# Weight loads as plain 128-partition reads, and ring loads placed in the space freed longest ago, in a two-layer decode kernel

## The chip, the cores and the metric

The kernel runs on one core of a Trainium2 chip. The metric is the device time of one execution in microseconds (us), the median of several runs. Of this kernel a profile gives the span from the first to the last instruction, some 2 to 3 us shorter than the device time of the same run (2660.8 for 2663.54 us before).

## The reference

Two layers of decoding with batch 2 and one new token. The same weights and the same caches serve both layers.

```python
x = A_x                                     # (2, 1, 576)
for layer in range(2):
    x = x + A(layernorm(x))                 # attention: 32 heads of 128, 16384 cached keys per head
    x = x + Bm(layernorm(x))                # mixer + MLP: x1 = x + shifted @ w2; x1 + gelu(ln(x1) @ w3) @ w4
# A:  q = x @ wq (576 x 4096); p = softmax(q K^T / sqrt(128)); o = p V; o @ wo (4096 x 576)
# Bm: w2 576 x 576, w3 576 x 4608, w4 4608 x 576; with one token the shifted term is zero
```

K and V hold 2 x 32 x 16384 x 128 bfloat16 values each: 64 "units" (batch x head) of 4.2 MB of K and 4.2 MB of V. They are read once in each layer, except for the last two units of layer 0, which stay in SBUF and are used first in layer 1. About 1.1 GB are moved in all.

## The kernel before

All loads of K, V, wq, w2, w3 and w4 go through one SBUF buffer of 12 slots of 16384 B a partition. The SP queue issues them in a fixed order. A K or V half (2 MB) fills one slot. A load may start when whatever lay in its place has been read. The place is chosen while the program is built, in program order:

```python
class Ring:                                             # (cut)
    def _place(self, n, aligned):
        p = self.at                                     # always the next address
        if aligned:
            p = -(-p // self.slot) * self.slot
        for _ in range(4 * len(self.live) + 4):
            if p + n > self.size:
                p = 0
            kept = [t for t in self.live if t["keep"] and t["off"] < p + n and p < t["off"] + t["n"]]
            if not kept:
                return p                                # skips tiles kept for layer 1, nothing else
            p = max(t["off"] + t["n"] for t in kept)
            ...
    def pump(self):
        while self.queue:
            key, n, src, aligned = self.queue[0]        # strictly in order
            p = self._place(n, aligned)
            if p is None:
                return
            under = [t for t in self.live if t["off"] < p + n and p < t["off"] + t["n"]]
            if not all(t["done"] for t in under):
                return                                  # that very place must be done
            ...
```

The matrices wq and w3 have 576 rows: four blocks of 128 and a tail of 64 rows. The tail is read as two loads, left columns to partitions 0 to 63, right columns to partitions 64 to 127:

```python
def krows(w, k, cut):
    n = w.shape[1]
    if k < self.KT - 1:
        ap = w[k * 128:(k + 1) * 128, :]
        return n, [lambda e, v: e.dma_start(v, ap)]
    a0, a1 = w[k * 128:D, 0:cut], w[k * 128:D, n - cut:n]
    return cut, [lambda e, v: e.dma_start(v[0:64, 0:cut], a0),
                 lambda e, v: e.dma_start(v[64:128, 0:cut], a1)]
...
# load order in each layer: K of unit i, then V of unit i-1, ...; at the end V 62, V 63, w3 (4 + tail), w4 (4 pieces),
# then (layer 0) wq of the next layer (4 + tail) and layer 1's K 61, K 60, V 61, K 59, V 60, ...
if l == 0 and i == 2:
    ap = self.w2.rearrange("(p r) n -> p (r n)", p=96)       # w2 on 96 partitions
```

Of the kernel before, what the change touches and what calls it, by code (L numbers as in the profile page):

```python
# [4 lines left out]
ALU = mybir.AluOpType  # L5
# [140 lines left out]
class Ring:  # L146
# [3 lines left out]
    def __init__(self, s, buf, size, slot):  # L150
        self.s, self.buf, self.size, self.slot = s, buf, size, slot
        self.at = 0
        self.live = []
        self.tiles = {}
        self.queue = []

# [3 lines left out]
    def _place(self, n, aligned):  # L160
        p = self.at
        if aligned:
            p = -(-p // self.slot) * self.slot
        for _ in range(4 * len(self.live) + 4):
            if p + n > self.size:
                p = 0
            kept = [t for t in self.live if t["keep"] and t["off"] < p + n and p < t["off"] + t["n"]]
            if not kept:
                return p
            p = max(t["off"] + t["n"] for t in kept)  # L170
            if aligned:
                p = -(-p // self.slot) * self.slot
        return None

    def pump(self):
        while self.queue:
            key, n, src, aligned = self.queue[0]
            p = self._place(n, aligned)
            if p is None:
                return  # L180
            under = [t for t in self.live if t["off"] < p + n and p < t["off"] + t["n"]]
            if not all(t["done"] for t in under):
                return
# [3 lines left out]
            t = dict(off=p, n=n, done=False, keep=False,  # L187
                     res=[("tile", key, part, self.s.n_dma) for part in range(len(src))])
            self.live.append(t)
            self.tiles[key] = t  # L190
            self.at = p + n
# [8 lines left out]
    def keep(self, key):  # L200
        self.tiles[key]["keep"] = True

    def done(self, key):
        t = self.tiles.pop(key)
        t["done"], t["keep"] = True, False
        self.pump()


class Decode:
# [6 lines left out]
    FJ = 4  # L216
    W4_PIECES = (3, 3, 2, 1)

    def __init__(self, nc, A_x, K, V, wq, wo, w2, w3, w4, out):
# [13 lines left out]
        self.FA0 = (self.FA + 1) // 2  # L233
# [12 lines left out]
        self.ring = Ring(self.s, self.ringbuf, self.NSLOT * self.slot, self.slot)  # L246
# [4 lines left out]
        self.cinv = sb("cinv", [128, 1], FP32)  # L251
        self.cone = sb("cone", [128, 1], FP32)
        self.ceps = sb("ceps", [128, 1], FP32)
# [4 lines left out]
        self.m1 = sb("m1", [128, 2], FP32)  # L258
        self.m2 = sb("m2", [128, 2], FP32)
        self.m = sb("m", [128, 2], FP32)  # L260
        self.bias = sb("bias", [128, 2], FP32)
# [11 lines left out]
        self.xnh = sb("xnh", [128, 2, B], BF16)  # L273
        self.xsum = sb("xsum", [128, KT, B], FP32)
        self.zero = sb("zero", [128, B], BF16)
        self.st = sb("st", [128, 2, B], FP32)
        self.var = sb("var", [128, B], FP32)
        self.rstd = sb("rstd", [128, B], FP32)
# [5 lines left out]
        self.gt = sb("gt", [128, MB], BF16)  # L284
# [20 lines left out]
    def plan(self):  # L305
        ring, B, H, D, TB = self.ring, self.B, self.H, self.D, self.TB
# [6 lines left out]
        def krows(w, k, cut):  # L313


            n = w.shape[1]
            if k < self.KT - 1:
                ap = w[k * 128:(k + 1) * 128, :]
                return n, [lambda e, v: e.dma_start(v, ap)]  # L319
            a0, a1 = w[k * 128:D, 0:cut], w[k * 128:D, n - cut:n]  # L320
            return cut, [lambda e, v: e.dma_start(v[0:64, 0:cut], a0),  # L321
                         lambda e, v: e.dma_start(v[64:128, 0:cut], a1)]
# [6 lines left out]
        def want_wq(l):  # L329
            for k in range(self.KT):  # L330
                n, src = krows(self.wq, k, H * 64)
# [6 lines left out]
        for l in range(2):  # L338
            order = self.order[l]
            skip = self.kept if l == 1 else set()  # L340
            for i, u in enumerate(order):
# [3 lines left out]
                if l == 0 and i == 2:  # L345
                    ap = self.w2.rearrange("(p r) n -> p (r n)", p=96)
                    ring.want(("w2",), 6 * D, [lambda e, v: e.dma_start(v[0:96, :], ap)])
# [3 lines left out]
            for k in range(self.KT):  # L351
                n, src = krows(self.w3, k, self.FA0 * self.FJ * 128)
# [26 lines left out]
    def release(self, kind, l, u, h):  # L379
        k = self.key(kind, l, u, h)  # L380
        if u in self.kept and l == 0:
            self.ring.keep(k)
        else:
            self.ring.done(k)


    def build(self):
# [3 lines left out]
        def consts(g):  # L391
# [4 lines left out]
            g.memset(self.xnh[:, :, :], 0.0)  # L396
            return g.memset(self.ident[:, :], 0.0)
        self.pool(consts, w=["ident", "consts", "xnh"])
# [8 lines left out]
                                           scalar2=None, op0=ALU.mult), r=["ident"], w=["identS"])  # L407
        xt = self.misc[:, :].bitcast(BF16)
# [59 lines left out]
    def k_matmuls(self, kind, l, out, pname, groups, over, pick):  # L468
# [4 lines left out]
        for k in range(self.KT):  # L473
# [10 lines left out]
            def halves(pe, w=w):  # L484
                for g in range(G - over):
                    for j in range(J):
                        m = g * J + j
                        at, rhs = out[:, m * B:(m + 1) * B], self.xnh[:, :, :]
                        if g < over:
                            at = bass.AP(tensor=at.tensor, offset=at.offset,  # L490
                                         ap=[list(at.ap[0]), [over * J * B, 2], [1, B]])
                        else:
                            at, rhs = out[:, (m + over * J) * B:(m + over * J + 1) * B], rhs[:, 1, :]
                        ins = pe.matmul(at, lhsT=pick(w, g, j), rhs=rhs, start=False, stop=True,
# [10 lines left out]
    def split_last(self):  # L505


        low = self.misc[0:64, 280:280 + self.B]
        self.pe(lambda pe: pe.matmul(low, lhsT=self.ident[64:128, 64:128], rhs=self.xn[64:128, self.KT - 1, :],
# [279 lines left out]
```

## Time and profile before

| | before |
|---|---|
| median of the runs | 2665.4 us |
| span of the profile | 2660.8 us |
| DMA rate in the steady state | 425 GB/s, one 2 MB load every 4.9 us |
| DMA rate over the span | 414 GB/s |

Lines of the page of the kernel before. "DMA" is the busy share of the 16 DMA engines in tenths in each of 40 slices, "GB/s" what they moved; the line of q8 has packets, MB and the share of 16 engines' time; the last line is the chain that ended last, by engine.

```profile
span 2660.8 us, 74381 instructions
...
DMA  9999999999999999999869999999999999999997
GB/s 388 425 426 426 425 424 426 426 426 425 425 425 426 425 425 425 425 425 425 338 249 425 424 427 424 426 425 425 425 426 425 426 425 425 427 425 425 425 425 293
...
q8 instruction: 270, 4.42, 0.7%
...
DMA 75%; DVE 24%; PE 1%; issue 0%; SPq 0%; ACT 0%; DVEq 0%
```

The DMA engines are busy nearly everywhere, so time is bytes over rate plus whatever slows or stops them. They move less at the start, in slices 20 and 21 (the layer boundary) and at the end.

The issues of the SP queue at the boundary of the kernel before: start and length in us, line, what is loaded, how many.

```profile
start us, us, engine line op out<-in xcount [idle before <-releaser]
...
1340.47 14.89 SPq L311 DMA_DIRECT2D ring<-in_A_k_cache_dram  x4
1394.23 0.81 SPq L311 DMA_DIRECT2D ring<-in_A_v_cache_dram  x2
1395.08 7.80 SPq L311 DMA_DIRECT2D ring<-in_A_k_cache_dram  x2
```

Four loads of K (units 61 and 60) are issued up to 1355 us. The next load, V of unit 61, is issued at 1394.23 us. Nothing is issued for 39 us. The waits of SP before (total us, times, longest) say for what:

```profile
engine line waited for: us in total, times, longest us
...
SPq L311 <- PE tps L606: 398.3, 76, 38.9
...
SPq L327 <- PE sps L480: 28.6, 2, 27.8
```

The longest wait for "PE tps" is 38.9 us: PE's transposes of K, that is, a K tile that has to be read before its slot can be taken. The last wait is w4 standing behind w3.

Four stretches of the kernel before: the first tail of wq, the first tail of w3 as the leading DMA engines reach it, the second tail of wq, and the hole. The columns at the end are the granted TensorE clock, the DMA share and GB/s.

```profile
core 0: us, PE busy (x) PEld busy (x) DVE busy (x) ACT busy (x) POOL busy (x), PEclk, DMA share, GB/s
11.00:17.00 6.00, 2.59 (x80) 2.37 (x80) 0.02 (x1) 0.00 (x0) 0.00 (x0) 1.00 1.03 350
1290.00:1302.00 12.00, 6.49 (x170) 5.97 (x167) 10.03 (x12) 6.24 (x10) 0.00 (x0) 0.78 0.99 358
1344.00:1356.00 12.00, 4.95 (x141) 4.56 (x138) 0.59 (x4) 0.28 (x1) 0.00 (x0) 0.50 1.02 324
1376.00:1394.00 18.00, 13.63 (x294) 13.13 (x291) 16.77 (x23) 10.20 (x19) 0.00 (x0) 0.62 0.07 18
```

The trace also records when each of the 16 engines finished its share of each load. I call the time from the first to the last engine's landing the spread. It is 0.4 us for the first load, 5 us at 200 us, 11 us at 550 us and 28 us at the end of layer 0; there, half of the engines lag by 24 us or more, five hardly at all and the other three by 2 to 13 us. In layer 1 it grows to 28 us again. The laggards' last landing is the moment that counts for the consumer.

### The profile page before, as it was taken

The page shows a single profiled execution, that of the slowest core. Times are in us where ns is not written, and L with a number is a line of the kernel's source. Part 1 is how long each engine was busy: PE and PEld are TensorE (multiplying, and loading weights), DVE is VectorE, ACT ScalarE, POOL GpSimd, SP SyncE. Part 2 cuts the span into 40 slices and gives each one's busy share as a digit, 9 for nine tenths or more (in the row PEclk, how much of TensorE's full clock was granted, in tenths as well). Part 3 has the DMA queues.
Part 4 walks back from the last instruction along what each step waited for, and adds up shares of the span by engine and source line. Part 5 has one row for each costly group of instructions (what it writes and reads, how often), then busy time and mean ns, then how long its engine had stood idle before and what let it go on. Part 6 is the DMA issues. An engine that isn't in the chain of part 4 may idle for free.

```text
span 2660.8 us, 74381 instructions
## 1 busy us (share of the span) xinstructions
PE 1570.0 (59%) x34580; PEld 1474.1 (55%) x34580; DVE 1994.1 (75%) x2753; ACT 1098.3 (41%) x1681; POOL 0.9 (0%) x11
## 2 busy tenths in 40 slices
PE   5556556655565655665567556556555555655655
PEld 5555555555555555555556555555555555555554
DVE  5777877777777777777568777777877777777774
ACT  3334434434434443443235434434434433443441
POOL 0000000000000000000000000000000000000000
PEclk7666666666666666666666666666666666666665
DMA  9999999999999999999869999999999999999997
GB/s 388 425 426 426 425 424 426 426 426 425 425 425 426 425 425 425 425 425 425 338 249 425 424 427 424 426 425 425 425 426 425 426 425 425 427 425 425 425 425 293
DMA packets 87085, 1102.65 MB, mean 414 GB/s; under 512 B 9108, under 2 KB 17304, under 8 KB 20216
## 3 DMA queue, kind: packets, MB, share of 16 engines
q1 hardware_dynamic: 78072, 1088.47, 97.0%
q10 hardware_dynamic: 8704, 9.44, 1.0%
q8 instruction: 270, 4.42, 0.7%
q14 instruction: 39, 0.32, 0.0%
HBM read 1097.87 MB, written 0.00 MB: 413 GB/s over the span
## 4 chain that ended last, share of the span: by engine, by line
DMA 75%; DVE 24%; PE 1%; issue 0%; SPq 0%; ACT 0%; DVEq 0%
DMA ring<-in_A_k_cache_dram 69%; DVE sd L639 15%; DVE prod L636 9%; DMA ring<-in_A_v_cache_dram 4%; DMA ring<-in_B_w_dram 1%; DMA ring<-in_A_wq_dram 1%; PE misc L657 0%; PE ops L684 0%; PE misc L519 0%; PE sps L480 0%; SPq L319 0%; PE misc L446 0%; PE misc L448 0%; DVE bias L659 0%; SPq L321 0%
## 5 line engine op out<-in xcount | busy, mean ns | idle before, releaser
L639 DVE TENSOR_REDUCE sd<-prod 128x8 f32<-128x1024 bf16 x1024 | 1249.4, 1220 | 35.4
L610 ACT ACTIVATE ktsb<-tps 128x1024 bf16<-128x1024 bf16 x1024 | 992.1, 1028 | 453.0 <-PE tps L606 447.9
L606 PE MATMUL tps<-ident,ring 128*128 128x128 bf16 x8192 | 830.2, 268 | 289.9 <-DMA ring<-in_A_k_cache_dram 289.9
L636 DVE TENSOR_TENSOR prod<-ring,qb 128x1024 bf16<-128x1024 bf16 x1024 | 699.1, 683 | 230.8 <-DMA ring<-in_A_k_cache_dram 220.1
L606 PEld LDWEIGHTS tps<-ident,ring 128*128 128x128 bf16 x8192 | 676.1, 123 | 314.5 <-DMA ring<-in_A_k_cache_dram 306.7
L684 PE MATMUL ops<-p,ring 128*128 128x1 bf16 x16384 | 469.5, 165 | 518.7 <-DMA ring<-in_A_v_cache_dram 509.3
L684 PEld LDWEIGHTS ops<-p,ring 128*128 128x128 bf16 x16384 | 448.4, 102 | 539.4 <-DMA ring<-in_A_v_cache_dram 529.2
L593 ACT ACTIVATE qb<-misc 128x128 bf16<-128x128 f32 x128 | 35.5, 278 | 1016.2 <-PE misc L591 1016.2
L624 PE MATMUL sps<-qt,ktsb 128*128 128x1 bf16 x8192 | 350.1, 166 | 92.3 <-ACT ktsb L610 83.8
L624 PEld LDWEIGHTS sps<-qt,ktsb 128*128 128x128 bf16 x8192 | 313.0, 102 | 132.5 <-ACT ktsb L610 131.0
L659 DVE TENSOR_REDUCE bias<-misc 128x1 f32<-128x128 f32 x128 | 37.3, 292 | 290.6 <-PE misc L657 290.6
L657 PE MATMUL misc<-identS,m 128*128 128x128 f32 x256 | 95.3, 476 | 34.8 <-DVE m L651 34.8
L657 PEld LDWEIGHTS misc<-identS,m 128*128 128x128 f32 x256 | 69.9, 333 | 36.7 <-DVE m L651 36.7
L519 PE MATMUL misc<-otn,wobuf 128*128 128x2 bf16 x320 | 13.6, 167 | 99.8 <-DVE otn L703 99.8
L519 PEld LDWEIGHTS misc<-otn,wobuf 128*128 128x128 bf16 x320 | 11.0, 105 | 102.7 <-DVE otn L703 102.7
L670 ACT ACTIVATE p<-sps,bias 128x64 bf16<-128x64 f32 x128 | 40.7, 318 | 23.5 <-DVE bias L659 23.5
L670 ACT ACTIVATE p<-sd,bias 128x64 bf16<-128x64 f32 x128 | 45.4, 355 | 0.0
L591 PE MATMUL misc<-ident,qt 128*128 128x128 bf16 x128 | 34.9, 272 | 11.7 <-DVE xa L713 7.8
L480 PE MATMUL sps<-xn,ring 128*128 128x2 bf16 x544 | 18.3, 169 | 16.7 <-DMA ring<-in_A_wq_dram 11.8
L647 DVE TENSOR_REDUCE m<-sps 128x1 f32<-128x64 f32 x128 | 27.6, 215 | 0.0
L670 ACT ACTIVATION_READ_ACCUMULATOR p<-sps,bias 128x1 f32 x128 | 27.1, 212 | 0.0
L480 PEld LDWEIGHTS sps<-xn,ring 128*128 128x128 bf16 x544 | 17.4, 112 | 17.6 <-DMA ring<-in_A_wq_dram 10.1
(70 smaller groups left out, 205.9 us busy)
## 6 DMA issues: line engine op xcount, KB each, us to landing
ring<-in_A_k_cache_dram SPq DMA_DIRECT2D x252, 2048.0 KB, 47.4
ring<-in_A_v_cache_dram SPq DMA_DIRECT2D x252, 2048.0 KB, 51.1
ring<-in_B_w_dram SPq DMA_DIRECT2D x10, 1152.0 KB, 48.1
wobuf<-in_A_wo_dram ACTq DMA_DIRECT2D x32, 288.0 KB, 15.3
ring<-in_A_wq_dram SPq DMA_DIRECT2D x8, 1024.0 KB, 11.6
ring<-in_B_w_dram SPq DMA_DIRECT2D x4, 1728.0 KB, 38.8
ring<-in_B_w_dram SPq DMA_DIRECT2D x4, 320.0 KB, 41.5
ring<-in_B_w_dram SPq DMA_DIRECT2D x2, 576.0 KB, 17.4
```

The costliest lines, as they stand in the source:

```text
L480: ins = pe.matmul(out[:, m * B:(m + 1) * B], lhsT=pick(w, g, j), rhs=self.xn[:, k, :], start=(k == 0 and m == 0), stop=False, skip_group_c ...
L591: self.pe(lambda pe: pe.matmul(self.misc[:, 0:128], lhsT=bcast(self.qt[:, u:u + 1], 128), rhs=self.ident[:, :], start=True, stop=True), r= ...
L593: self.act(lambda a: a.activation(out=self.qb[q][:, :], in_=self.misc[:, 0:128], func=ACT.Copy), r=["P:misc"], w=[f"qb{q}"])
L606: ins = pe.transpose(self.tps[b][:, j * 128:(j + 1) * 128], kt[:, (j0 + j) * 128:(j0 + j + 1) * 128], self.ident[:, :])
L610: self.act(lambda a: a.activation(out=self.ktsb[k][:, :, :].rearrange("p a b -> p (a b)"), in_=self.tps[b][:, :], func=ACT.Copy), r=[f"P:t ...
L624: ins = pe.matmul(self.sps[sp][:, col:col + 1], lhsT=self.ktsb[k][:, j, :], rhs=self.qt[:, u:u + 1], start=True, stop=True)
L636: self.dve(lambda v: v.tensor_tensor(out=self.prod[d][:, :, :], in0=k3, in1=bcast_mid(self.qb[q][:, :], self.CH), op=ALU.mult), r=[*res, f ...
L639: self.dve(lambda v: v.tensor_reduce(out=self.sd[q][:, o:o + self.CH], in_=self.prod[d][:, :, :], axis=AX.X, op=ALU.add), r=[f"prod{d}"], ...
L657: self.pe(lambda pe: pe.matmul(self.misc[:, 128:256], lhsT=bcast(self.m[:, q:q + 1], 128), rhs=self.identS[:, :], start=True, stop=True), ...
L659: self.dve(lambda v: v.tensor_reduce(out=self.bias[:, q:q + 1], in_=self.misc[:, 128:256], axis=AX.X, op=ALU.max, negate=True), r=["P:misc ...
L670: self.act(lambda a, c0=c0, c1=c1, src=src, part=part: a.activation(out=self.p[q][:, c0:c1], in_=src, func=ACT.Exp, bias=self.bias[:, q:q ...
L684: ins = pe.matmul(self.ops[g][:, col:col + 1], lhsT=vt[:, j * 128:(j + 1) * 128], rhs=self.p[q][:, h * self.TB + j:h * self.TB + j + 1], s ...
```

## The change

Two intents. First, a load is placed in whatever free space was freed longest ago, instead of the next address. Second, all weights are read as plain 128-partition loads: the 64-row tails as two partitions a row, w2 as 128 partitions x 4 rows and a rest of 64 rows (74 KB, still on 64 partitions), and w3 and w4 in groups of 3 for 4, so that the halves of the tail come out even. A selector matrix and a parity vector spread the last 64 values of the activations to the new tail layout. The rest makes room in SBUF.

```diff
-class Ring:
+class Arena:
     def _place(self, n, aligned):
-        p = self.at
-        ... (next address, skipping kept tiles)
+        best = None
+        if aligned:
+            starts = range(0, self.size - n + 1, self.slot)
+        else:
+            starts = sorted({0} | {t["off"] for t in self.live} | {t["off"] + t["n"] for t in self.live})
+        for p in starts:
+            if p + n > self.size:
+                continue
+            under = [t for t in self.live if t["off"] < p + n and p < t["off"] + t["n"]]
+            if all(t["done"] for t in under):
+                age = max([t["done"] for t in under], default=0)
+                if best is None or age < best[0]:
+                    best = (age, p, under)
+        return best
...
-    FJ = 4
-    W4_PIECES = (3, 3, 2, 1)
+    FJ = 3
+    W4_PIECES = (5, 4, 2, 1)
...
             if k < self.KT - 1:
                 ap = w[k * 128:(k + 1) * 128, :]
-                return n, [lambda e, v: e.dma_start(v, ap)]
-            a0, a1 = w[k * 128:D, 0:cut], w[k * 128:D, n - cut:n]
-            return cut, [lambda e, v: e.dma_start(v[0:64, 0:cut], a0),
-                         lambda e, v: e.dma_start(v[64:128, 0:cut], a1)]
+            else:
+                n //= 2
+                ap = w[k * 128:D, :].rearrange("r (c n) -> (r c) n", c=2)
+            return n, [lambda e, v: e.dma_start(v, ap)]
...
-                    ap = self.w2.rearrange("(p r) n -> p (r n)", p=96)
-                    ring.want(("w2",), 6 * D, [lambda e, v: e.dma_start(v[0:96, :], ap)])
+                    n = 128 * (self.KT - 1)
+                    w2a, w2b = self.w2[0:n, :].rearrange("(p r) n -> p (r n)", p=128), self.w2[n:D, :]
+                    ring.want(("w2",), KT * D, [lambda e, v: e.dma_start(v[:, 0:(KT - 1) * D], w2a),
+                                                lambda e, v: e.dma_start(v[0:64, (KT - 1) * D:KT * D], w2b)])
... (selector, parity, small tiles merged, matmuls of the tail)
```

More of the change, by code (lines that the diff above doesn't have):

```diff
@@ L143, in bcast_mid @@
     return bass.AP(tensor=ap.tensor, offset=ap.offset, ap=[list(ap.ap[0]), [0, n], list(ap.ap[1])])
-class Ring:
+class Arena:
     def __init__(self, s, buf, size, slot):
         self.s, self.buf, self.size, self.slot = s, buf, size, slot
-        self.at = 0
         self.live = []
@@ L155, in __init__ @@
         self.queue = []
+        self.n_done = 0
     def want(self, key, n, src, aligned=True):
@@ L160, in _place @@
     def _place(self, n, aligned):
-        p = self.at
+        best = None
         if aligned:
-            p = -(-p // self.slot) * self.slot
-        for _ in range(4 * len(self.live) + 4):
+            starts = range(0, self.size - n + 1, self.slot)
+        else:
+            starts = sorted({0} | {t["off"] for t in self.live} | {t["off"] + t["n"] for t in self.live})
+        for p in starts:
             if p + n > self.size:
-                p = 0
-            kept = [t for t in self.live if t["keep"] and t["off"] < p + n and p < t["off"] + t["n"]]
-            if not kept:
-                return p
-            p = max(t["off"] + t["n"] for t in kept)
-            if aligned:
-                p = -(-p // self.slot) * self.slot
-        return None
+                continue
[5 more added lines that the diff above has]
+        return best
     def pump(self):
@@ L177, in pump @@
             key, n, src, aligned = self.queue[0]
-            p = self._place(n, aligned)
-            if p is None:
+            best = self._place(n, aligned)
+            if best is None:
                 return
-            under = [t for t in self.live if t["off"] < p + n and p < t["off"] + t["n"]]
-            if not all(t["done"] for t in under):
-                return
+            _, p, under = best
             self.queue.pop(0)
@@ L186, in pump @@
             self.live = [t for t in self.live if t not in under]
-            t = dict(off=p, n=n, done=False, keep=False,
-                     res=[("tile", key, part, self.s.n_dma) for part in range(len(src))])
+            t = dict(off=p, n=n, done=0, res=[("tile", key, part, self.s.n_dma) for part in range(len(src))])
             self.live.append(t)
             self.tiles[key] = t
-            self.at = p + n
             view = self.buf[:, p:p + n]
@@ L198, in get @@
         return self.buf[:, t["off"]:t["off"] + t["n"]], t["res"]
-    def keep(self, key):
-        self.tiles[key]["keep"] = True
     def done(self, key):
         t = self.tiles.pop(key)
-        t["done"], t["keep"] = True, False
+        self.n_done += 1
+        t["done"] = self.n_done
         self.pump()
@@ L232, in __init__ @@
         self.FA = self.MT // self.FJ
-        self.FA0 = (self.FA + 1) // 2
         assert sum(self.W4_PIECES) == self.FA
@@ L245, in __init__ @@
         self.ringbuf = sb("ring", [128, self.NSLOT * self.slot], BF16)
-        self.ring = Ring(self.s, self.ringbuf, self.NSLOT * self.slot, self.slot)
+        self.ring = Arena(self.s, self.ringbuf, self.NSLOT * self.slot, self.slot)
         self.ktsb = [sb(f"ktsb{i}", [128, self.CH, 128], BF16) for i in range(self.NKT)]
@@ L250, in __init__ @@
         self.identS = sb("identS", [128, 128], FP32)
-        self.cinv = sb("cinv", [128, 1], FP32)
-        self.cone = sb("cone", [128, 1], FP32)
-        self.ceps = sb("ceps", [128, 1], FP32)
         self.qt = sb("qt", [128, self.U], BF16)
@@ L257, in __init__ @@
         self.sd = [sb(f"sd{i}", [128, self.TB], FP32) for i in range(2)]
-        self.m1 = sb("m1", [128, 2], FP32)
-        self.m2 = sb("m2", [128, 2], FP32)
-        self.m = sb("m", [128, 2], FP32)
-        self.bias = sb("bias", [128, 2], FP32)
+        small = sb("small", [128, 11 + 4 * B], FP32)
+        self.cinv, self.cone, self.ceps = small[:, 0:1], small[:, 1:2], small[:, 2:3]
+        self.m1, self.m2, self.m, self.bias = (small[:, 3 + 2 * i:5 + 2 * i] for i in range(4))
+        self.st = small[:, 11:11 + 2 * B].rearrange("p (a b) -> p a b", a=2)
+        self.var, self.rstd = small[:, 11 + 2 * B:11 + 3 * B], small[:, 11 + 3 * B:11 + 4 * B]
         self.wobuf = sb("wobuf", [128, self.GH, self.D], BF16)
@@ L273, in __init__ @@
         self.xnh = sb("xnh", [128, 2, B], BF16)
+        self.sel = sb("sel", [128, 128], BF16)
+        self.par = sb("par", [128, 2], FP32)
         self.xsum = sb("xsum", [128, KT, B], FP32)
         self.zero = sb("zero", [128, B], BF16)
-        self.st = sb("st", [128, 2, B], FP32)
-        self.var = sb("var", [128, B], FP32)
-        self.rstd = sb("rstd", [128, B], FP32)
         MB = self.MT * B
@@ L283, in __init__ @@
         self.zr = g1[:, 0:MB]
-        self.gt = sb("gt", [128, MB], BF16)
+        self.gt = self.prod[0][:, :, :].rearrange("p a b -> p (a b)")[:, 6 * MB:7 * MB]
         self.rows = self.prod[1][:, :, :].rearrange("p a b -> p (a b)")[:, 0:self.D]
@@ L305, in plan @@
     def plan(self):
-        ring, B, H, D, TB = self.ring, self.B, self.H, self.D, self.TB
+        ring, B, H, D, KT, TB = self.ring, self.B, self.H, self.D, self.KT, self.TB
         def kv(src, u, h):
@@ L311, in kv, with krows @@
             return [lambda e, v: e.dma_start(v, ap)]
-        def krows(w, k, cut):
+        def krows(w, k):
             n = w.shape[1]
@@ L330, in want_wq @@
             for k in range(self.KT):
-                n, src = krows(self.wq, k, H * 64)
+                n, src = krows(self.wq, k)
                 ring.want(("wq", l, k), n, src, aligned=(k == 0 and l == 0))
@@ L351, in plan @@
             for k in range(self.KT):
-                n, src = krows(self.w3, k, self.FA0 * self.FJ * 128)
+                n, src = krows(self.w3, k)
                 ring.want(("w3", l, k), n, src, aligned=(k == 0))
@@ L379, in release @@
     def release(self, kind, l, u, h):
-        k = self.key(kind, l, u, h)
-        if u in self.kept and l == 0:
-            self.ring.keep(k)
-        else:
-            self.ring.done(k)
+        if l == 1 or u not in self.kept:
+            self.ring.done(self.key(kind, l, u, h))
     def build(self):
@@ L395, in consts @@
             g.memset(self.zero[:, :], 0.0)
-            g.memset(self.xnh[:, :, :], 0.0)
             return g.memset(self.ident[:, :], 0.0)
-        self.pool(consts, w=["ident", "consts", "xnh"])
+        self.pool(consts, w=["ident", "consts"])
         self.pool(lambda g: g.affine_select(out=self.ident[:, :], in_=self.ident[:, :], compare_op=ALU.not_equal,
@@ L407, in build @@
                                            scalar2=None, op0=ALU.mult), r=["ident"], w=["identS"])
+        up = self.ident[64:128, 64:128]
+        self.dve(lambda v: v.tensor_copy(out=self.sel[64:128, :].rearrange("p (r c) -> p r c", c=2),
+                                         in_=bass.AP(tensor=up.tensor, offset=up.offset,
+                                                     ap=[list(up.ap[0]), [1, 64], [0, 2]])), r=["ident"], w=["sel"])
+        self.dve(lambda v: v.tensor_reduce(out=self.par[:, :],
+                                           in_=self.ident[:, :].rearrange("p (r c) -> p c r", c=2), axis=AX.X,
+                                           op=ALU.add), r=["ident"], w=["par"])
         xt = self.misc[:, :].bitcast(BF16)
@@ L466, in layernorm, with k_matmuls @@
                  r=["xc", "rstd"], w=[dname])
-    def k_matmuls(self, kind, l, out, pname, groups, over, pick):
+    def k_matmuls(self, kind, l, out, pname, groups, pick):
         G, J = groups
@@ L484, in halves @@
             def halves(pe, w=w):
-                for g in range(G - over):
+                for g in range(G // 2):
                     for j in range(J):
                         m = g * J + j
-                        at, rhs = out[:, m * B:(m + 1) * B], self.xnh[:, :, :]
-                        if g < over:
-                            at = bass.AP(tensor=at.tensor, offset=at.offset,
-                                         ap=[list(at.ap[0]), [over * J * B, 2], [1, B]])
-                        else:
-                            at, rhs = out[:, (m + over * J) * B:(m + over * J + 1) * B], rhs[:, 1, :]
-                        ins = pe.matmul(at, lhsT=pick(w, g, j), rhs=rhs, start=False, stop=True,
+                        at = out[:, m * B:(m + 1) * B]
+                        at = bass.AP(tensor=at.tensor, offset=at.offset,
+                                     ap=[list(at.ap[0]), [G // 2 * J * B, 2], [1, B]])
+                        ins = pe.matmul(at, lhsT=pick(w, g, j), rhs=self.xnh[:, :, :], start=False, stop=True,
                                         skip_group_check=True)
@@ L505, in split_last @@
     def split_last(self):
-        low = self.misc[0:64, 280:280 + self.B]
-        self.pe(lambda pe: pe.matmul(low, lhsT=self.ident[64:128, 64:128], rhs=self.xn[64:128, self.KT - 1, :],
-                                     start=True, stop=True), r=["xn", "ident"], w=["P:misc"])
-        def copies(v):
-            v.tensor_copy(out=self.xnh[64:128, 1, :], in_=self.xn[64:128, self.KT - 1, :])
-            return v.tensor_copy(out=self.xnh[0:64, 0, :], in_=low)
-        self.dve(copies, r=["P:misc", "xn"], w=["xnh"])
+        B = self.B
+        twice = self.misc[:, 280:280 + B]
+        self.pe(lambda pe: pe.matmul(twice, lhsT=self.sel[64:128, :], rhs=self.xn[64:128, self.KT - 1, :],
+                                     start=True, stop=True), r=["xn", "sel"], w=["P:misc"])
+        self.dve(lambda v: v.tensor_tensor(
+            out=self.xnh[:, :, :], in0=bcast_mid(twice, 2),
+            in1=bass.AP(tensor=self.par[:, :].tensor, offset=self.par[:, :].offset,
+                        ap=[list(self.par[:, :].ap[0]), [1, 2], [0, B]]), op=ALU.mult),
+            r=["P:misc", "par"], w=["xnh"])
     def d_matmuls(self, pe, out, w, rhs, first, last):
@@ L523, in q_proj @@
     def q_proj(self, l):
-        self.k_matmuls("wq", l, self.sps[1], "P:sps1", (self.H, 1), self.H // 2,
+        self.k_matmuls("wq", l, self.sps[1], "P:sps1", (self.H, 1),
                        lambda w, g, j: w[:, g * 128:(g + 1) * 128])
@@ L538, in mlp @@
         na = 128 * self.FJ
-        self.k_matmuls("w3", l, z, "P:sps0", (self.FA, self.FJ), self.FA - self.FA0,
+        self.k_matmuls("w3", l, z, "P:sps0", (self.FA, self.FJ),
                        lambda w, g, j: spread(w[:, g * na + j:g * na + j + 1], 128, self.FJ))
@@ L549, in mlp @@
         self.dve(lambda v: v.tensor_tensor(out=self.gt[:, :], in0=self.zr, in1=z, op=ALU.mult),
-                 r=["prod1", "P:sps0", "zu", "prod0"], w=["gt"])
+                 r=["prod1", "P:sps0", "zu", "ze"], w=["prod0"])
         h2 = self.misc[:, 256:256 + KT * B]
@@ L561, in f @@
                 return ins
-            self.pe(f, r=[*res, "gt"], w=["P:misc"])
+            self.pe(f, r=[*res, "prod0"], w=["P:misc"])
             self.ring.done(("w4", l, c))
@@ L575, in f @@
         def f(pe):
-            for r in range(6):
-                ins = self.d_matmuls(pe, out, w[0:96, r * self.D:(r + 1) * self.D], self.zero[0:96, :], r == 0, r == 5)
+            for r in range(KT):
+                n = 128 if r < KT - 1 else 64
+                ins = self.d_matmuls(pe, out, w[0:n, r * self.D:(r + 1) * self.D], self.zero[0:n, :], r == 0,
+                                     r == KT - 1)
             return ins
```

## The prediction

> **What bounds the kernel now.** The DMA engines. The page's slices show a DMA share of 9 tenths in nearly all of 40, at about 425 GB/s; the chain that ended last is 75% DMA. A 2 MB K or V half lands every 4.9 us. The span (2660.8 us) is bytes over rate plus the holes.
>
> (a) The 16 engines are not equal. One load's landings on its 16 engines spread over 0.4 us at the start and 28 us at the end of layer 0; about half of the engines lag. The queue "instruction" made 271 packets of 16384 B, 1.07 us each, one per 9.9 us; I take them as the cause[...]. The lagging engines set the time; they are busy without a break to 2656.8 us at the end.
>
> (b) Their only real idle is at the layer boundary. The timeline of SP shows that after four K loads (1340 to 1355 us) the next load (V 61) is issued only at 1394.2 us, after K 61's transposes: the wait "PE tps, longest 38.9 us". The ring insists on the next address, K 61's slot, while slots of the kept units 63 and 62 are already free (K 63 halves at about 1362 and 1370, K 62 first half 1377.6, V 63 about 1380). The last of the four K loads landed at 1369 (fast engines) to 1375 us (slow). DMA share is near 0 from 1375 to 1395 us.
>
> **What the change does.**
> 1. Placement: V 61 goes into K 63's halves (1362, 1370), K 59 into K 62's (1378, 1386), V 60 into V 63's (1380). The slow engines, busy to 1375, then always have a load waiting. Gain 20 us less 1 us of a wo load that ran in the hole: **-19 us**, all critical, as DMA stays the limit (compute needs 16.45 us a unit there, DMA 19.6). In the steady state releases come in the order of loads, so nothing changes.
> 2. Tails: each 64-partition half of wq's tail took 1.2 us for 256 KB, of w3's 1.25 us for 320 KB, half the usual rate.[...] As one 128-partition load, 8 packets of 4096 or 4608 B (0.16, 0.18 us) an engine: saves about 1.1 us four times. w2 with 128 for 96 partitions: about -0.3. **-4.5 us.**
> 3. w4 in runs of 3456 B for 4608 B (0.180 us; estimate 0.138): **+0.25 us a layer.** PE work is unchanged within 1 us.
>
> Before w3 is consumed, w4's second piece still has no room (8 of 12 slots are kept), so the wait at 1300 to 1325 us stays, hidden behind the slow engines.
>
> **Prediction.** 2665.6 - 19 - 4.5 + 0.5 = about 2642 us; range 2634 to 2652. Faster by over 2% (under 2612): 0.01, as all idle of the slow engines is less than that. Within 2%: 0.98. Slower: 0.01.
>
> **What would show it.** The V load after the boundary's K loads issued near 1360 us, PE's 38.9 us wait gone; DMA share near 1 from 1355 to 1430; spread at the end still near 30 us; no 5120-byte packets; w3's tail landing 1.4 us after the load before it.
>
> **What would make it wrong.** Slots freed later than I read, so that part of the hole stays (2650); fetch delays on other engines; odd-sized w4 pieces blocking the queue.

The sum comes to 2642.6 us (2665.6 - 19 - 4.5 + 0.5), put as about 2642. The -4.5 us rests on the times read from the trace alone (256 KB in 1.2 us is 218 GB/s, 320 KB in 1.25 us is 262, for 425 in the steady state), and the -0.3 us for w2 is an estimate.

## The result

| | before | after |
|---|---|---|
| median of 4 runs | 2665.38 us | 2628.03 us |
| range | 2664.26 to 2665.82 | 2627.94 to 2628.21 |
| ratio after / before, 95% interval | | 0.9861 (0.9843 to 0.9878) |
| span of the profile | 2660.8 us | 2626.2 us |

A ratio is the mean time of one kernel's fast runs over that of the other's of the same rounds, so it is not quite the ratio of the medians. The kernel is 37 us faster: within 2%, as predicted, but below the predicted range (2634 to 2652). The profiled run of the kernel before took 2663.54 us, 1.8 us under the median, so the two traces below show 34.6 of the 37 us.

The same lines of the page, after:

```profile
span 2626.2 us, 74358 instructions
...
DMA  9999999999999999999999999999999999999997
GB/s 405 425 426 425 425 424 426 426 426 425 425 425 426 425 425 425 425 425 427 383 386 425 425 425 425 426 425 425 425 426 425 425 425 424 427 425 425 425 425 308
...
q8 instruction: 270, 4.42, 0.7%
...
DMA 64%; DVE 18%; PE 8%; another core or an unknown queue 7%; ACT 2%; issue 1%; SPq 0%; ACTq 0%; DVEq 0%
```

Slices 20 and 21 went from 338 and 249 GB/s to 383 and 386. The first slice gained too. The instruction packets are the same.

SP's issues at the boundary after:

```profile
start us, us, engine line op out<-in xcount [idle before <-releaser]
...
1333.52 12.20 SPq L302 DMA_DIRECT2D ring<-in_A_k_cache_dram  x4
1352.48 7.86 SPq L302 DMA_DIRECT2D ring<-in_A_v_cache_dram  x2
1368.02 8.76 SPq L302 DMA_DIRECT2D ring<-in_A_k_cache_dram  x2
```

V of unit 61 now follows the K loads by 7 us instead of 39. Its place is K 63's first half, as predicted. The waits after:

```profile
engine line waited for: us in total, times, longest us
...
SPq L302 <- PE tps L600: 291.7, 68, 8.3
...
SPq L317 <- PE sps L475: 34.5, 2, 34.0
```

The longest wait for "PE tps" fell from 38.9 to 8.3 us; the wait of w4 behind w3 grew from 27.8 to 34.0 us and costs nothing, as the lagging engines are busy all that time. The stretches after, the last one over the times of the hole before:

```profile
core 0: us, PE busy (x) PEld busy (x) DVE busy (x) ACT busy (x) POOL busy (x), PEclk, DMA share, GB/s
11.00:17.00 6.00, 2.87 (x81) 2.46 (x81) 0.22 (x1) 0.28 (x1) 0.00 (x0) 1.00 1.04 436
1288.00:1300.00 12.00, 6.97 (x203) 6.46 (x201) 10.83 (x12) 5.72 (x10) 0.00 (x0) 0.78 0.98 408
1336.00:1346.00 10.00, 5.05 (x149) 4.66 (x150) 0.93 (x6) 0.50 (x2) 0.00 (x0) 0.50 1.02 430
1376.00:1394.00 18.00, 12.48 (x259) 11.83 (x259) 16.77 (x22) 9.47 (x14) 0.00 (x0) 0.59 0.97 402
```

Against the four lines of before: 436 GB/s for 350 at the first tail of wq, 408 for 358 at that of w3, 430 for 324 at the second tail of wq, and 402 for 18 where the hole was (402 and not 425 because the leading engines wait a few us for K 62's second half; the laggards don't).

Where the time came from can be read from the landings. This table has the last engine's landing of the same loads in both traces, in us from the start, and the difference so far.

| load | before | after | difference |
|---|---|---|---|
| tail of wq, layer 0 | 16.3 | 14.7 | -1.6 |
| second load after w2 | 71.0 | 67.9 | -3.1 |
| V 63, second half (end of attention 0) | 1312.7 | 1308.4 | -4.3 |
| tail of w3, layer 0 | 1327.2 | 1320.9 | -6.3 |
| tail of wq, layer 1 | 1354.3 | 1344.7 | -9.6 |
| fourth K load of layer 1 | 1375.2 | 1365.8 | -9.4 |
| K 59, second half | 1417.7 | 1386.2 | -31.5 |
| tail of w3, layer 1 | 2644.5 | 2609.7 | -34.8 |
| last piece of w4 | 2656.8 | 2622.3 | -34.5 |

The hole gave 22 us, between the fourth K load and K 59. The other 12 us came at the places where tails and w2 are loaded. That holds for the step to V 63 too: through the attention of layer 0 the difference stays at -2.8 to -3.2 us, and the last landings lose their 1.3 us only at 1297 to 1303 us, just as the leading engines cross w3's tail (1295 to 1298 us) while the laggards still load V; the first landings stay at -2.8. The prediction had 19 and 4.5.

My theory after the result: the hole is the ring's doing and was sized about right; the tails were mis-sized, because a 64-partition load costs more than the time it takes itself. Rivals: placement also pays for the rest (w4 and wq issued earlier at the boundary); or the smaller w4 pieces do.

### The profile page after: what moved, and what is told of

Read it like the earlier page. It is cut to its first block, busy times and chain, and to the rows that moved or that the text cites. A ratio compares the mean times of both kernels' runs of the same rounds, so it can differ in the third digit from the quotient of the medians.

```text
span 2626.2 us, 74358 instructions
## 1 busy us (share of the span) xinstructions
PE 1567.1 (60%) x34571; PEld 1472.1 (56%) x34571; DVE 1993.5 (76%) x2751; ACT 1098.0 (42%) x1681; POOL 0.8 (0%) x10
## 4 chain that ended last, share of the span: by engine, by line
DMA 64%; DVE 18%; PE 8%; another core or an unknown queue 7%; ACT 2%; issue 1%; SPq 0%; ACTq 0%; DVEq 0%
DMA ring<-in_A_k_cache_dram 34%; DMA ring<-in_A_v_cache_dram 26%; DVE sd L633 11%; DVE prod L630 6%; PE ops L678 4%; DMA ring<-in_B_w_dram 2%; PE tps L600 2%; ACT ktsb L604 2%; PE sps L618 1%; PE misc L651 1%; DMA ring<-in_A_wq_dram 1%; ACT p L664 0%; PE misc L585 0%; PE misc L511 0%
## 5 line engine op out<-in xcount | busy, mean ns | idle before, releaser
L633 DVE TENSOR_REDUCE sd<-prod 128x8 f32<-128x1024 bf16 x1024 | 1249.3, 1220 | 35.4
L653 DVE TENSOR_REDUCE small<-misc 128x1 f32<-128x128 f32 x128 | 37.3, 292 | 280.6 <-PE misc L651 280.6
L651 PE MATMUL misc<-identS,small 128*128 128x128 f32 x256 | 95.6, 477 | 52.6 <-DVE small L645 52.6
L651 PEld LDWEIGHTS misc<-identS,small 128*128 128x128 f32 x256 | 69.7, 332 | 55.8 <-DVE small L645 55.8
L664 ACT ACTIVATE p<-sps,small 128x64 bf16<-128x64 f32 x128 | 40.5, 316 | 23.2 <-DVE small L653 23.2
L664 ACT ACTIVATE p<-sd,small 128x64 bf16<-128x64 f32 x128 | 45.3, 354 | 0.0
L585 PE MATMUL misc<-ident,qt 128*128 128x128 bf16 x128 | 34.8, 272 | 14.2 <-DVE xa L707 7.8
L641 DVE TENSOR_REDUCE small<-sps 128x1 f32<-128x64 f32 x128 | 27.6, 215 | 0.0
L664 ACT ACTIVATION_READ_ACCUMULATOR p<-sps,small 128x1 f32 x128 | 27.1, 211 | 0.0
L643 DVE TENSOR_REDUCE small<-sd 128x1 f32<-128x64 f32 x128 | 26.7, 209 | 0.0
L664 ACT ACTIVATION_READ_ACCUMULATOR p<-sd,small 128x1 f32 x128 | 26.4, 206 | 0.0
```

The source lines that it names most:

```text
L585: self.pe(lambda pe: pe.matmul(self.misc[:, 0:128], lhsT=bcast(self.qt[:, u:u + 1], 128), rhs=self.ident[:, :], start=True, stop=True), r= ...
L633: self.dve(lambda v: v.tensor_reduce(out=self.sd[q][:, o:o + self.CH], in_=self.prod[d][:, :, :], axis=AX.X, op=ALU.add), r=[f"prod{d}"], ...
L641: self.dve(lambda v: v.tensor_reduce(out=self.m1[:, q:q + 1], in_=self.sps[q][:, 0:n], axis=AX.X, op=ALU.max), r=[f"P:sps{q}"], w=[f"m1{q}"])
L651: self.pe(lambda pe: pe.matmul(self.misc[:, 128:256], lhsT=bcast(self.m[:, q:q + 1], 128), rhs=self.identS[:, :], start=True, stop=True), ...
L653: self.dve(lambda v: v.tensor_reduce(out=self.bias[:, q:q + 1], in_=self.misc[:, 128:256], axis=AX.X, op=ALU.max, negate=True), r=["P:misc ...
L664: self.act(lambda a, c0=c0, c1=c1, src=src, part=part: a.activation(out=self.p[q][:, c0:c1], in_=src, func=ACT.Exp, bias=self.bias[:, q:q ...
```

## The experiments

Eighteen kernels ran. All gave the correct result. "Before" on the same chip was 2664.5 to 2665.8 us in all jobs. Differences between kernels below are differences of medians, partly of jobs on different chips; so one of 1 us says nothing. The runs of one kernel lay mostly within 1.5 us, at most 4.2 us, of each other.

### Placement alone, loads alone

The kernel before with only the class that places loads exchanged:

```diff
-        self.ring = Ring(self.s, self.ringbuf, self.NSLOT * self.slot, self.slot)
+        self.ring = Arena(self.s, self.ringbuf, self.NSLOT * self.slot, self.slot)
```

> The kernel before with the new placement alone (tails, w2 and w4 as before). My theory: placement gives the hole at the layer boundary and nothing else: 22 us (the step from the fourth K landing to the third next load was 37.6 us before and 15.4 us after), so about 2643.5 us, and the excess packet time around the half-partition tails stays as it was. Rival (placement also pays for the rest, by earlier w4 and wq loads): about 2633 us or less.

Measured: 2643.28 us, ratio to before 0.9922 (0.9907 to 0.9937), so 21.5 us faster than the 2664.76 of before. The theory's number was met; placement does not pay for the other 15 us.

The kernel after with the old ring, so the plain loads alone (the reverse of the diff above, on the kernel after):

> The kernel after with the old ring: plain loads (wq, w3, w2, w4 in threes) alone. My theory after the result: the tails were mis-sized in the prediction, they give 12 us because a half-partition load slows the 16 engines twice when the engines are out of step, so about 2653 us, with the boundary hole of about 20 us still there. Prediction on record: 4 us, so 2661 us.

Measured: 2632.72 us, ratio 0.9881 (0.9866 to 0.9895). That is 32 us faster than before, far more than either number. SP's issues in that run show why:

```profile
start us, us, engine line op out<-in xcount [idle before <-releaser]
...
1333.83 12.23 SPq L307 DMA_DIRECT2D ring<-in_A_k_cache_dram  x4
1353.23 7.45 SPq L307 DMA_DIRECT2D ring<-in_A_v_cache_dram  x2
1370.74 2.37 SPq L307 DMA_DIRECT2D ring<-in_A_k_cache_dram  x2
1384.29 9.28 SPq L307 DMA_DIRECT2D ring<-in_A_v_cache_dram  x2
```

The hole is nearly gone with the old ring too: V 61 is issued at 1353 us, and a smaller gap, from 1373 to 1384 us, remains. With the new sizes of tails and w4 pieces, the next address after the fourth K load is the slot of a kept tile that is soon free; with the old sizes it was the slot just given to K 61, which is read only after units 63 and 62. I replayed the placement rule step by step, and it gives the same: V 61 over K 61 with the old sizes, V 61 over K 63 with the new ones. So the 39 us wait was not a property of the ring as such but of the ring with those sizes. Either half of the change removes most of it, and the two halves' gains (21.5 and 32) cannot be added. What is safe to say is the gain in one order: placement first 21.5 us, then the loads 15.3 us (2643.28 to 2628.03).

### Which loads the 15 us come from

Three runs undo one load each in the kernel after, for both layers. Old tail of wq (w3 in the same way):

```diff
             else:
                 n //= 2
+                if old:                                 # True for wq alone
+                    a0, a1 = w[k * 128:D, 0:n], w[k * 128:D, n:2 * n]
+                    return n, [lambda e, v: e.dma_start(v[0:64, :], a0), lambda e, v: e.dma_start(v[64:128, :], a1)]
                 ap = w[k * 128:D, :].rearrange("r (c n) -> (r c) n", c=2)
```

(with the old copy of the activations' last rows into a tile of its own beside it)

> The kernel after with only wq's last 64 rows as two 64-partition halves again (both layers). Prediction on record: 2 times 1.1 us. From the landings: 1.2 us at the start, where the pair stands behind wq's own loads, and 4 to 5 us at the boundary, so 5 to 6 us: about 2633.5 us.

Measured: 2632.03 us, ratio 0.9876 (0.986 to 0.9893): 4.0 us over the kernel after, less than the 5 to 6 expected. The landings put 1.2 to 1.4 us of it at the start of layer 0 and 3.0 at the boundary.

> The same for w3's last 64 rows (both layers). Prediction on record: 2 times 1.1 us. From the landings 3 to 3.5 us in each layer: 6 to 7 us, about 2634.5 us.

Measured: 2635.91 us, ratio 0.9892 (0.9878 to 0.9907): 7.9 us over the kernel after, more than expected.

Old w2:

```diff
-                    w2a, w2b = self.w2[0:n, :].rearrange("(p r) n -> p (r n)", p=128), self.w2[n:D, :]
+                    ap = self.w2.rearrange("(p r) n -> p (r n)", p=96)
```

> The kernel after with w2 on 96 partitions again. Prediction on record: 0.3 us. From the excess of packet time there (2.1 us an engine before, 0.5 after): 1.6 us, about 2629.6 us. If the three sum to much less than the 15 us between placement alone and the whole change, something else in the change pays, such as w4 in threes.

Measured: 2630.83 us, ratio 0.9873 (0.9858 to 0.9888): 2.8 us over the kernel after, where 1.6 was expected. By the landings 2.1 us of it are lost right at w2; the loads at the boundary are placed as in the kernel after. The three sum to 14.7 us of the 15.3, so the loads that leave partitions out pay for nearly all of it, and w4 in threes neither pays nor costs anything that shows.

### Neighbouring partitions or rows

The dear thing could be the 64 partitions side by side or a load of 64 rows as such. Here, eight extra tails of w3 are loaded in layer 0 at units 50 to 57, each in its own slot and each read by one small matmul: as halves, as plain loads, and as halves on every second partition.

```diff
# shortened
+                if l == 0 and i in (50, ..., 57):
+                    ring.want(("x", i), 2304, [lambda e, v: e.dma_start(v[0:64, :], self.w3[512:576, 0:2304]),
+                                               lambda e, v: e.dma_start(v[64:128, :], self.w3[512:576, 2304:4608])])
# plain twin:   one dma_start(v, w3[512:576, :] as two partitions a row)
# combs:        v[0:128:2, :] and v[1:128:2, :] for the two halves
```

> The same eight pairs of halves at units 50 to 57 of layer 0, where the engines are 23 to 26 us out of step. My theory (both groups of engines are slowed when either one crosses the half-partition load, so the lagging group pays twice): 2.0 to 2.5 us a pair dearer than its plain twin, 16 to 20 us in all. Rival (a pair costs the same in step or not, as the prediction had it): 9 to 10 us.

Measured: 2677.24 us, ratio to before 1.0047 (1.0032 to 1.0062).

> The plain twin at units 50 to 57: 11 us of bytes on 2628 us, so 2639 to 2642 us; the time should be that of the early plain twin within 3 us.

Measured: 2641.86 us, ratio 0.9914 (0.9899 to 0.9929). So eight pairs of halves are 35.4 us dearer than eight plain loads, 4.4 us a pair: above both numbers expected.

> As the run with late pairs of halves (2677 us), but each 64-row load goes to every second partition (even ones, then odd ones) instead of the lower and the upper 64. [...] If a load of 64 rows is dear as such: 2677 us.

(If the neighbouring partitions are what costs, I expected a time close to the plain twin's, 2642 to 2648 us.)

Measured: 2641.58 us, ratio 0.9911 (0.9896 to 0.9926), the time of the plain twin. The same 64-row loads with the same packets cost nothing extra here (0.3 us less than the plain twin) when each goes to every second partition. The windows below are the stretch of 100 us with most of the extra loads (columns as in the windows above). First the run with halves:

```profile
core 0: us, PE busy (x) PEld busy (x) DVE busy (x) ACT busy (x) POOL busy (x), PEclk, DMA share, GB/s
1000.00:1100.00 100.00, 47.78 (x1061) 44.04 (x1061) 63.86 (x92) 34.09 (x53) 0.00 (x0) 0.64 1.01 366
```

The same window of the run with plain loads:

```profile
1000.00:1100.00 100.00, 58.77 (x1256) 55.62 (x1256) 73.35 (x104) 42.90 (x65) 0.00 (x0) 0.64 1.01 425
```

The same window of the run with combs:

```profile
1000.00:1100.00 100.00, 57.87 (x1256) 54.20 (x1256) 73.49 (x104) 42.55 (x65) 0.00 (x0) 0.67 1.01 424
```

The DMA share is 1.01 in all three, GB/s 366, 425 and 424. So a high DMA share does not tell how much is moved. With halves, the mean packet of a K or V load grew from 0.615 us to about 1.1 us in the worst stretches of 4 us: the halves slow the K and V loads beside them. So it is the 64 neighbouring partitions that are dear, not the 64 rows (2677.24 us against 2641.58). Why they are was not shown.

### Why a pair costs 1.2 us in one place and 4 in another

My first idea was that engines out of step (spread 25 us) pay twice. The same loads at units 3 to 10, where the spread is 2 to 5 us:

> The kernel after with eight more loads at units 3 to 10 of layer 0, each the last 64 rows of w3 as two 64-partition halves (the old form); the engines are nearly in step there (spread 2 to 5 us). Read against its twin with plain loads at the same units. If a pair of halves costs what it cost at the start of the kernel before, it is 1.1 to 1.3 us a pair dearer: 9 to 10 us in all. The prediction on record has the same number.

Measured: 2673.05 us, ratio 1.0031 (1.0014 to 1.0048).

> The twin: the same eight loads at units 3 to 10 as plain 128-partition loads, two partitions a row. 8 times 590 KB at 425 GB/s is 11 us: about 2639 to 2641 us, if the shifted placement at the boundary costs nothing (the probe run showed that it can cost 2 or 3 us).

Measured: 2642.80 us, ratio 0.9917 (0.9902 to 0.9932). The difference is 30.3 us, 3.8 us a pair, nearly as much as late. The theory as I had put it, with the size of the lag deciding, fell: a spread of 2 to 5 us costs nearly as much as one of 23 to 26.

Then four pairs between the first four K loads:

> The kernel after with four pairs of w3-tail halves between the first four K loads, where the engines are within 0.4 to 2 us of each other and the neighbours are 16384-byte packets as in the late runs. Against its plain twin. If a pair is cheap only because engines are in step: 1.1 to 1.4 us a pair, 5 us in all. If it is the neighbouring big packets that make it dear: 3.8 us a pair as at units 3 to 10, 15 us in all.

Measured: 2646.72 us, ratio 0.9929 (0.9914 to 0.9944).

> Its twin with plain 128-partition loads: four loads of 590 KB, 1.4 us each, so about 2634 us.

Measured: 2634.11 us, ratio 0.9883 (0.9867 to 0.99). The difference is 12.6 us, 3.15 us a pair: dear here too. That spoke for the neighbours' big packets. The landings of the plain twin show, however, that one engine is already 2 us late there, after an instruction packet at 14.8 us. So I changed only the neighbours' packets, in the runs with late pairs: K and V in runs of 4096 B for 16384.

```diff
-            ap = src[b, hh].rearrange("(t p j) d -> t p (j d)", t=2, p=128)[h]
-            return [lambda e, v: e.dma_start(v, ap)]
+            ap = src[b, hh].rearrange("(t a p j) d -> t p a (j d)", t=2, a=4, p=128)[h]
+            return [lambda e, v: e.dma_start(v.rearrange("p (a m) -> p a m", a=4), ap)]
```

> The late pairs of halves, with K and V read in runs of 4096 bytes instead of 16384 (keys and values reordered alike, so the result is the same). Against its plain twin. [...] If the size of the neighbours' packets does not matter: 35 us in all, as with big packets.

(If the size of the neighbours' packets is what makes a pair dear, I expected clearly less than 4.4 us a pair: 1.4 to 2.7 us, 11 to 22 us in all.)

Measured: 2782.16 us, ratio 1.0438 (1.0422 to 1.0453).

> Its plain twin. Runs of 4096 bytes take 0.159 us each in the trace for 0.615 us of a 16384-byte one, so four cost 0.636 us, 3.4% more: about 2641.9 times 1.032, 2725 us, if DMA stays the limit.

Measured: 2750.28 us, ratio 1.0321 (1.0304 to 1.0338). The difference is 31.9 us, 4.0 us a pair for 4.4 with big packets. The neighbours' packet size is not the main reason. (In passing: runs of 4096 B cost the kernel 4.1%, a little more than I worked out.)

The last run puts the four pairs ahead of everything, where no engine lags yet:

> The kernel after with the four extra pairs of halves as the very first ring loads, ahead of wq, where all 16 engines start together. Their plain twin cost 2634.1 us with the same bytes between the first K loads; the place of plain loads should not matter. If a pair is cheap as long as no engine lags at all: 1.1 to 1.4 us a pair over the twin, 2638.5 to 2640 us, and the four pairs land within about 11 us of the first. If a pair is as dear here as at units 3 to 10: 3.2 to 3.8 us a pair, about 2647 to 2649 us.

Measured: 2638.14 us, ratio 0.99 (0.9884 to 0.9917): 4.0 us over the plain twin of the start, 1.0 us a pair. So pairs were cheap where all 16 engines passed them together, and three times as dear where one engine lagged by about 2 us, little more than a half load's own length. That the lag is what decides is not fully separated: in this last run the pairs also have other pairs as neighbours, not K loads. Two things speak for the lag. The first tail of wq (1.2 to 1.4 us when undone) has a plain load on either side and was cheap as well. And in the run with pairs between the first K loads, from wq's tail to the end of the first pair, the first landing took 1.5 us more than in the plain twin, the mean of the 16 engines 1.6 us more, and the late engine's 3.1 us more: with the same neighbours, the engines in step paid half of what the late one paid.

Of the cause this much is measured: in step a pair cost 1.0 us (the last run), and out of step K and V packets beside the half loads took longer too (0.87 us instead of 0.615 beside w3's tail in the trace of before, 1296 to 1300 us). My reading, which fits these numbers but is not shown packet by packet: out of step an engine pays twice, once in its own half load and once with a K or V packet while others are in theirs.

### What makes the engines lag

The prediction took the instruction packets as the cause. A first try added do-nothing instructions on PE:

```diff
+        def pad(pe):
+            for _ in range(64):
+                ins = pe.nop()
+            return ins
+        self.pe(pad)
```

> The kernel after with 64 more do-nothing instructions on PE before each V half's matmuls (16384 in all, 64 more blocks of 256). If instruction fetches make the lag: 334 instead of 270 packets on the instruction queue, spread of the landings at the end of each layer up from 27 us by about a quarter to 33 us, and the whole run about 12 us longer[...]. If the lag has another cause: spread 27 us, time within 2 us of 2628.

(The packets themselves took 1.07 us each in the trace of before. The 256 instructions a block are measured in the second try below.)

Measured: 2628.19 us, ratio 0.9864 (0.9847 to 0.988), with 270 instruction packets and 74358 instructions, exactly those of the kernel after. The instructions never reached the chip, so this run says nothing.

The second try doubles PE's transposes, each into the same place:

```diff
-            for j in range(self.CH):
+            for j in sorted(2 * list(range(self.CH))):
                 ins = pe.transpose(self.tps[b][:, j * 128:(j + 1) * 128],
```

> The kernel after with every transpose on PE done twice into the same place: 16384 more PE instructions that reach the chip, 64 blocks of 256. (The do-nothing instructions of the first try did not reach it: same 270 packets, same 74358 instructions.) If instruction fetches make the lag: 334 packets on the instruction queue, spread at the end of each layer 33 us for 27, time about 12 us longer, 2640 us, though PE and ACT work off the critical path. If not: spread 27 us and time within 2 us of 2628.

Measured: 2640.44 us, ratio 0.9907 (0.9892 to 0.9921): 12.4 us over the kernel after. Two lines of its page:

```profile
span 2638.2 us, 90742 instructions
...
q8 instruction: 334, 5.47, 0.8%
```

64 more packets, as expected, against 270 after, for 16384 more instructions (90742 against 74358): one packet for every 256. The largest spread at the end of the layers is 33.8 and 34.1 us, against 27.8 and 28.8. A rival, that twice the transposes make PE itself hold up the loads, doesn't fit the landings: through layer 0 the last landings fall back step by step, 5.7 us by its end, while the first landings stay within 1 us of those of the kernel after and end 0.5 us earlier. So more PE instructions cost time here although PE was busy for only 60% of the span of the kernel after: 16384 of them brought 64 more packets on the queue "instruction", whose share of the 16 DMA engines' time went from 0.7% to 0.8%, and 12.4 us. An estimate from this run: 32 more packets a layer gave 6 us more spread, so the kernel's own 135 a layer would give 25 of its 28 us.

Which engines lag? A load of 8 rows, to every fourth of 32 partitions; its landings came from eight engines:

```diff
# shortened
+                if l == 0 and i in (20, 50):
+                    ring.want(("x", i), TB * 128, [8 rows of a K half -> e.dma_start(v[0:32:4, :], f[0:32:4, :])])
```

> The kernel after with two more loads in layer 0 (at units 20 and 50) that read 8 rows to every fourth of 32 partitions, so that 8 DMA engines carry them. It only asks which engines: if the 8 that it uses are the ones that run ahead, its landings spread under 12 us and come with the first landings of the neighbouring loads; if they are the lagging ones, they come with the last; if mixed, the spread is that of the neighbours (about 11 us at unit 20, 24 us at unit 50). Time within 3 us of 2628.

Measured: 2631.72 us in its one run (state unknown, and 3.7 us slower than the kernel after; by the landings that arises at the layer boundary, where loads were placed otherwise: V loads come 0.6 us later before it and 3.6 us later after it). At unit 50, six of the eight engines landed at 1005.8 to 1014.1 us, two at 1025.2 and 1026.9, when the spread of whole loads was about 22 us. The eight are mixed: six that run ahead, two that lag. So this load does not spare the laggards. The same probe at unit 52 could not be built: the odd slot left no two free slots side by side for the first w4 piece (17280 B), and the queue stopped for good (a replay of the placement rule shows it). Placement by age can fragment.

No experiment pointed to a version faster than the kernel after. In it the laggards are never idle between the start and the last piece of w4, as far as the landings show, so what is left, as far as I see, is fewer bytes, fewer instruction packets or a more even split over the engines, for which I found no means.

## Why the prediction was wrong

- **What bounds the kernel: right.** The lagging DMA engines set the time, and instruction packets make them lag (12.4 us for 64 more packets, spread 28 to 34 us).
- **The hole: right in mechanism, 3 us too small.** Predicted -19 us, measured 22 us in the landings and 21.5 us with placement alone. The missing part is the restart: before, the first load after the hole was issued at 1394.2 us and landed at 1402.3, 8.1 us later, while a load in a full queue lands 4.9 us after the one before it. I had counted idle time only up to the first packets at 1395 us. What I also did not see: the old ring with the new sizes would nearly have closed the hole as well.
- **The tails and w2: this step failed.** The prediction put it as "saves about 1.1 us four times. w2 with 128 for 96 partitions: about -0.3. -4.5 us." Measured by undoing each: wq 4.0 us for 2.2, w3 7.9 for 2.2, w2 2.8 for 0.3, together 14.7 us. That halves on 64 neighbouring partitions are dear was right (eight pairs cost 35.4 us more than plain loads, and nothing more on every second partition: 2641.58 us for 2641.86); why they are was not shown. The size was wrong because I counted only the halves' own duration (1.2 us a half at wq's first tail, where all engines are in step, and 1.25 us at w3's, read on the leading engines) and nothing for what they do to the loads beside them. With all engines in step a pair costs 1.0 to 1.4 us more than a plain load; everywhere else it cost 3.0 to 4.4 us, because the loads beside it are slowed too. I could have seen it: in the trace of before, K and V packets beside the tail of w3 (1296 to 1300 us) take 0.87 us on average instead of 0.615.
- **w4 in runs of 3456 B: right.** Estimated 0.138 us a packet, 0.135 us in the trace after; no cost shows.
- **Signs to look for:** V 61 issued at 1352.5 us (predicted near 1360), DMA share near 1 through the boundary, spread still 27 to 28 us, w3's tail landing 1.4 us after the load before it (1319.5 and 1320.9 us), no packets of 5120 B. All came true; none of them would have shown the mis-sized term, as I named no sign for what the tails do to their neighbours.
- **The chances:** "within 2%" was right (ratio 0.9861); the range from 2634 us was too narrow at its lower end by 6 us.

## What to carry to other kernels

In a kernel bound by DMA, look at GB/s and at the length of packets, not at the DMA share: here, with pairs of loads to the lower and the upper 64 partitions, the share stayed at 1.01 while GB/s fell from 425 to 366 and the mean K or V packet took up to 1.1 us for 0.615; a pair cost 4.4 us more than a plain load where it cost 1.0 us as the first loads, and nothing more with the same rows on every second partition (2641.58 us for 2641.86). Size such a term where it happens, from the packets around it, not from its own duration alone. And when a queue waits long for one slot while others are free, ask which sizes brought it there: a first-in-first-out ring can be good or bad by luck of its sizes.
